# Two tokens per partition in the first six blocks: loads in rows of 384 bytes, products as 64-row tiles

## The chip, the core and the metric

The kernel runs on one core of a Trainium2 chip. The core has engines that run side by side, each with its own queue of instructions in a fixed order: PE (TensorE, matrix products into PSUM), DVE (VectorE), ACT (ScalarE), POOL (GpSimd) and SP (SyncE, which here only issues DMAs). 16 DMA engines move data between the device memory (HBM) and the on-chip memory (SBUF). The metric is the device time of one execution in microseconds (us).

## What is computed

A gated linear attention with a recurrent state, and a two-layer network on its output:

```python
for t in range(S):                       # per batch (4) and head (8); S = 768 tokens, head_dim 48
    state = alpha[t][:, None] * state + outer(k[t], v[t])
    y[t] = q[t] @ state
x = y, laid out as (4 * 768) tokens by (8 * 48) = 384 columns
h = x @ w_in                             # 384 -> 2048
g = s * relu(h) ** 2 + b
out = g @ w_out                          # 2048 -> 384
```

q, k, v and alpha are float32 of shape (4, 8, 768, 48): one head's token is a row of 48 values, 192 bytes. The output is 3072 by 384, float32.

## The kernel before

The 3072 tokens are cut into 24 blocks of C = 128 (`NBLK`), six to a batch (`NCH`). A block lies with one token on each partition and its eight heads along the free axis, in four pairs of heads (`NP`). Within a block the recurrence is written as matrix products. For block n:

- `load_a`, `load_k`, `load_q`, `load_v` (L121 to L131) fetch the block's four tensors, one DMA each of 128 x 8 pieces of 192 bytes, into rings of 8 buffers (`NLD`).
- `ln` (ACT) takes the logarithm of alpha, and `cum` (L208) sums it over the tokens with one matmul by an upper triangular matrix `U_bf`; for the first blocks (n < 5) four tiny matmuls with `ones_c` give the block's total. ACT takes the exponentials, `bi_sb` and `b_sb` (L221, L222), and for the first blocks the decay over the whole block, `blast`. For later blocks `decay` fetches that row by way of HBM (L230, L232).
- `qk` (DVE) scales k and q by them; `tr` transposes both on PE (8 matmuls), and DVE copies the result to `qkT`.
- `amat` (L254) makes the scores: 8 matmuls, one per head, 48 rows high, 128 keys by 128 queries, into two PSUM tiles. DVE multiplies each by a causal mask (`mask4`) into `am_a`, `am_b`.
- `yp` (L274) makes y: in blocks that have a predecessor in their batch 4 matmuls of q with the state `sd_sb`, then 8 matmuls of scores with v (`v_bf`, cast by POOL in `vcast`), into `y_ps`; and 4 matmuls of k with v into `p_ps`, for the new state. ACT copies y to `y_bf`.
- `st` / `state` (L329): DVE adds the state products to the decayed old state (`t1_sb`, named t_sb in the profile), POOL multiplies it by the decay (`sd_sb`, `sc_sb`).
- `xt` transposes y on PE, ACT copies it to `xd_all`.
- `mp` (L354) is the first layer in four pieces of 12 matmuls into `h_ps`, `rl` the relu on ACT, `sq` the square on DVE (`gt_all`), `mm2` (L394) the second layer in four pieces of 4 matmuls into `o_ps`. Blocks 0 to 12 are kept on the chip (`keep_sb`) until the bias is known, then stored; the later ones are stored from `out_sb`.

The order on every engine is written out by hand. A list gives the first blocks' steps one after the other (L512), with `busy`, matmuls whose result nobody reads, between them (28 in all, 128 x 512 each). They read `U_bf` and `mask4`. From block 4 on each step has a position, `at(pos, ...)`, with a block every 8 positions. The list interleaves attention of blocks 0 to 4 with the casts of the weights (`win`, `wout`) and the first layers of blocks 0 to 3.

The DMAs of the start stand in SP's queue in the order of L445 to L461: all of blocks 0 and 1, the four quarters of w_in with alpha and k of blocks 2 and 3 between them, the four parts of w_out, then blocks 4 to 7. `early` lets ACT issue q and v of blocks 2 and 3; in ACT's order that of block 2 stands behind the exponentials of block 1. Every DMA issued by SP or ACT counts on one of eight semaphores, which are dealt out in rotation over both queues; a DMA is issued only when the last one on its semaphore has landed. At the front POOL builds the triangular matrices and the masks (a memset and a select each), and DVE clears buffers.

Of the kernel before, what the change touches and what calls it, by code (L numbers as in the profile page):

```python
# [14 lines left out]
def kernel(  # L15
# [25 lines left out]
    UNITS = 5  # L41
    assert sum(GROUPS) == NBLK
# [13 lines left out]
    y_ps = ps.tile([128, 512], FP32, name="y_ps")  # L56
    p_ps = ps.tile([128, 512], FP32, name="p_ps")
# [11 lines left out]
    ones_c = sb.tile([128, 1], BF16, name="ones_c")  # L69
    ones_f = sb.tile([128, 128], FP32, name="ones_f")  # L70
# [46 lines left out]
    def src(t, n):  # L117
        b, c = n // NCH, n % NCH
        return t[b, :, c * C : (c + 1) * C, :].rearrange("h s d -> s h d")

    def load_a(n, eng=None):  # L121
        (eng or nc.sync).dma_start(out=al_sb[n % NLD], in_=src(alpha, n))  # L122

    def load_q(n, eng=None):
        (eng or nc.sync).dma_start(out=q_sb[n % NLD], in_=src(q, n))  # L125

    def load_k(n, eng=None):
        (eng or nc.sync).dma_start(out=k_sb[n % NLD], in_=src(k, n))  # L128

    def load_v(n, eng=None):  # L130
        (eng or nc.sync).dma_start(out=v_sb[n % NLD], in_=src(v, n))  # L131
# [70 lines left out]
    def ln(n):  # L202
        nc.scalar.activation(out=la_sb[n % 2][:, :, 0:48], in_=al_sb[n % NLD], func=AF.Ln)  # L203

    def vcast(n):
        nc.gpsimd.tensor_copy(out=v_bf[n % 3], in_=v_sb[n % NLD])  # L206

    def cum(n):  # L208
        la = la_sb[n % 2]
        nc.tensor.matmul(out=cum_ps, lhsT=U_bf, rhs=la[:, :, 0:48], start=True, stop=True)  # L210
        if n < NCH - 1:
# [25 lines left out]
    def qk(n):  # L237
        nc.vector.tensor_tensor(out=kb_sb[n % 3][:, :, 0:48], in0=k_sb[n % NLD], in1=bi_sb[n % 2], op=ALU.mult)  # L238
        nc.vector.tensor_tensor(out=qb_sb[n % 2][:, :, 0:48], in0=q_sb[n % NLD], in1=b_sb[n % 2], op=ALU.mult)  # L239

    def tr(n):
        for x, t in ((0, qb_sb[n % 2]), (1, kb_sb[n % 3])):
            for p in range(NP):
                nc.tensor.transpose(  # L244
                    out=t_ps[0:112, x, p, :],
# [8 lines left out]
    def amat(n):  # L254
        qkT = qkT_sb[n % 2]
        for p in range(NP):
# [9 lines left out]
        for e in range(2):  # L266
            nc.vector.tensor_tensor(out=am_sb[e][n % 2], in0=a_ps[e], in1=mask4, op=ALU.mult)  # L267
# [5 lines left out]

    def yp(n):  # L274
        c = n % NCH
# [53 lines left out]
    def state(n):  # L329
        c = n % NCH  # L330
        if c == 0:
            nc.vector.tensor_copy(out=t1_sb[0:112], in_=pst[0:112])
        else:
            nc.vector.tensor_tensor(out=t1_sb[0:112], in0=pst[0:112], in1=sc_sb[0:112], op=ALU.add)  # L334
# [256 lines left out]
```

## Time and profile before

| | |
|---|---|
| time, median of 3 runs | 200.46 us (200.07 to 201.05) |
| span of the profiled execution, first to last instruction | 198.2 us |
| what lies around the span, against the three runs | 1.9 to 2.9 us |
| PE busy | 185.2 us (93% of the span), 2440 matmuls |
| DVE busy | 150.8 us (76%) |
| ACT busy | 118.8 us (60%) |
| POOL busy | 64.2 us (32%) |
| DMA | 113,454 packets, 30.33 MB, 106,627 of them under 512 bytes |
| a load (192 KB), from issue to landing, median | 3.2 (alpha) to 4.9 us (v) |
| PE busy from 20 to 58 us | 33.7 of 38 us |
| PE busy from 60 to 120 us | 59.9 of 60 us |

The profile's own time for the profiled execution is its span; what the runs' times hold beyond it, before the first instruction and after the last, is not in the profile. A group's "busy" adds the lengths of instructions that overlap on PE, so the price of a matmul in a row of matmuls is read from the distance of two starts. An engine named with a q (SPq, ACTq) is the queue that issues its DMAs.

### The profile page before, as it was taken

The page shows a single profiled execution, that of the slowest core. Times are in us where ns is not written, and L with a number is a line of the kernel's source. Part 1 is how long each engine was busy: PE and PEld are TensorE (multiplying, and loading weights), DVE is VectorE, ACT ScalarE, POOL GpSimd, SP SyncE. Part 2 cuts the span into 40 slices and gives each one's busy share as a digit, 9 for nine tenths or more (in the row PEclk, how much of TensorE's full clock was granted, in tenths as well). Part 3 has the DMA queues.
Part 4 walks back from the last instruction along what each step waited for, and adds up shares of the span by engine and source line. Part 5 has one row for each costly group of instructions (what it writes and reads, how often), then busy time and mean ns, then how long its engine had stood idle before and what let it go on. Part 6 is the DMA issues. An engine that isn't in the chain of part 4 may idle for free.

```text
span 198.2 us, 6120 instructions
## 1 busy us (share of the span) xinstructions
PE 185.2 (93%) x2440; PEld 145.3 (73%) x2440; DVE 150.8 (76%) x296; ACT 118.8 (60%) x243; POOL 64.2 (32%) x96
## 2 busy tenths in 40 slices
PE   1999899988899999999999999999999999999994
PEld 1566587754577688888878877878888877877783
DVE  5467777867466779789877996989987999998532
ACT  3245668381675765766766677666575665664650
POOL 5142251611120136326500633623700851652000
PEclk9999999999999999999999999999999999999999
DMA  7999999999999384693968846958947953122212
GB/s 125 189 342 232 314 283 369 199 177 193 187 172 195 60 142 86 101 159 64 195 84 148 134 68 120 159 93 193 229 87 164 161 176 112 41 82 81 87 37 79
DMA packets 113454, 30.33 MB, mean 153 GB/s; under 512 B 106627, under 2 KB 111890, under 8 KB 113426
## 3 DMA queue, kind: packets, MB, share of 16 engines
q1 hardware_dynamic: 109262, 29.15, 73.7%
q10 hardware_dynamic: 4164, 0.79, 2.8%
q8 instruction: 19, 0.31, 0.7%
q14 instruction: 9, 0.07, 0.1%
HBM read 25.19 MB, written 4.74 MB: 151 GB/s over the span
## 4 chain that ended last, share of the span: by engine, by line
PE 68%; SPq 15%; DMA 10%; DVE 3%; ACT 1%; issue 1%; ACTq 0%; DVEq 0%
PE h_ps L365 25%; PE o_ps L402 25%; DMA q_sb<-in_q_dram 8%; SPq L128 5%; PE ct_ps L244 5%; SPq L147 4%; PE a_ps L259 3%; SPq L125 3%; SPq L122 2%; PE ct_ps L210 2%; PE y_ps L287 2%; PE h_ps L312 2%; DMA al_sb<-in_alpha_dram 2%; SPq L131 1%; PE a_ps L425 1%; PE y_ps L278 1%
## 5 line engine op out<-in xcount | busy, mean ns | idle before, releaser
L379 ACT ACTIVATE r_sb<-h_ps 128x512 bf16<-128x512 f32 x94 | 55.8, 597 | 39.2 <-PE h_ps L365 37.6
L365 PE MATMUL h_ps<-xd_all,w_in_bf 128*128 128x128 bf16 x1128 | 74.8, 219 | 1.5 <-ACT r_sb L379 1.1
L365 PEld LDWEIGHTS <-w_in_bf 128*128 128x128 bf16 x1152 | 69.3, 98 | 8.4 <-issue 2.3
L402 PE MATMUL o_ps<-w_out_bf,gt_all 128*128 128x384 bf16 x336 | 68.5, 326 | 1.4 <-DVE w_out_bf L160 0.7
L386 DVE TENSOR_TENSOR gt_all<-r_sb 128x512 bf16<-128x512 bf16 x96 | 45.3, 484 | 26.5 <-ACT r_sb L379 25.8
L339 POOL TENSOR_TENSOR sd_sb<-t_sb,blast 48x192 bf16<-48x192 f32 x40 | 22.5, 563 | 103.5 <-DVE t_sb L334 67.3
L402 PEld LDWEIGHTS <-gt_all 128*128 128x128 bf16 x368 | 32.5, 98 | 17.4 <-issue 1.8
L343 POOL TENSOR_TENSOR sc_sb<-t_sb,blast 112x384 f32<-112x384 f32 x16 | 21.8, 1362 | 1.3
L206 POOL CAST v_bf<-v_sb 128x384 bf16<-128x384 f32 x24 | 17.7, 744 | 12.9 <-DMA v_sb<-in_v_dram 12.7
L318 ACT ACTIVATE xd_all<-h_ps 128x384 bf16<-128x384 bf16 x24 | 11.8, 490 | 15.5 <-PE h_ps L312 15.5
L249 DVE COPY qkT<-ct_ps 112x1024 bf16<-112x1024 bf16 x24 | 16.4, 685 | 4.8 <-PE ct_ps L244 4.7
L238 DVE TENSOR_TENSOR kb_sb<-k_sb,bi_sb 128x384 bf16<-128x384 f32 x24 | 13.7, 569 | 8.3 <-ACT bi_sb L221 8.2
L267 DVE TENSOR_TENSOR am_a<-a_ps,mask 128x512 bf16<-128x512 f32 x24 | 16.4, 683 | 3.1 <-PE a_ps L259 3.1
L239 DVE TENSOR_TENSOR qb_sb<-q_sb,b_sb 128x384 bf16<-128x384 f32 x24 | 16.7, 694 | 0.0
L267 DVE TENSOR_TENSOR am_b<-a_ps,mask 128x512 bf16<-128x512 f32 x24 | 16.3, 681 | 0.0
L221 ACT ACTIVATE bi_sb<-ct_ps 128x384 f32<-128x384 f32 x24 | 11.7, 487 | 5.2 <-PE ct_ps L213 3.9
L305 ACT ACTIVATE y_bf<-y_ps 128x384 bf16<-128x384 f32 x24 | 11.7, 488 | 4.9 <-PE y_ps L287 4.8
L203 ACT ACTIVATE la_sb<-al_sb 128x384 bf16<-128x384 f32 x24 | 12.4, 516 | 3.6 <-DMA al_sb<-in_alpha_dram 3.6
L210 PE MATMUL ct_ps<-la_sb,U_bf 128*128 128x384 bf16 x24 | 8.2, 340 | 4.6 <-ACT la_sb L203 4.6
L222 ACT ACTIVATE b_sb<-ct_ps 128x384 f32<-128x384 f32 x24 | 11.9, 494 | 0.0
L244 PEld LDWEIGHTS <-qb_sb 128*112 128x112 bf16 x96 | 8.5, 136 | 4.4 <-DVE qb_sb L239 3.2
L259 PE MATMUL a_ps<-qkT 48*128 48x128 bf16 x192 | 10.2, 226 | 1.0 <-DVE qkT L249 0.4
(66 smaller groups left out, 195.0 us busy)
## 6 DMA issues: line engine op xcount, KB each, us to landing
al_sb<-in_alpha_dram SPq DMA_DIRECT2D x24, 192.0 KB, 3.2
k_sb<-in_k_dram SPq DMA_DIRECT2D x24, 192.0 KB, 3.6
q_sb<-in_q_dram SPq DMA_DIRECT2D x22, 192.0 KB, 4.7
v_sb<-in_v_dram SPq DMA_DIRECT2D x22, 192.0 KB, 4.9
w_in_st<-in_moe_w_in_dram SPq DMA_DIRECT2D x4, 768.0 KB
w_out_st<-in_moe_w_out_dram SPq DMA_DIRECT2D x4, 768.0 KB
out_dram<-w_in_st SPq DMA_DIRECT2D x13, 192.0 KB, 2.6
out_dram<-out_sb SPq DMA_DIRECT2D x10, 192.0 KB, 3.4
```

What stands on the lines that cost most here:

```text
L206: nc.gpsimd.tensor_copy(out=v_bf[n % 3], in_=v_sb[n % NLD])
L239: nc.vector.tensor_tensor(out=qb_sb[n % 2][:, :, 0:48], in0=q_sb[n % NLD], in1=b_sb[n % 2], op=ALU.mult)
L244: nc.tensor.transpose(out=t_ps[0:112, x, p, :], in_=t.rearrange("a h d -> a (h d)")[:, 128 * p : 128 * p + 112], identity=ident,)
L249: nc.vector.tensor_copy(out=qkT_sb[n % 2][0:112].rearrange("a x p t -> a (x p t)"), in_=t_ps[0:112].rearrange("a x p t -> a (x p t)"),)
L259: nc.tensor.matmul(out=a_ps[e][:, p, :], lhsT=qkT[r0 : r0 + 48, 1, p, :], rhs=qkT[r0 : r0 + 48, 0, p, :], start=True, stop=True,)
L267: nc.vector.tensor_tensor(out=am_sb[e][n % 2], in0=a_ps[e], in1=mask4, op=ALU.mult)
L339: nc.gpsimd.tensor_tensor(out=sd[r, :, d], in0=t1_sb[r, :, d], in1=bl[r].to_broadcast([48, NP, 48]), op=ALU.mult)
L343: nc.gpsimd.tensor_tensor(out=sc_sb[0:112], in0=t1_sb[0:112], in1=bl[0:112].to_broadcast([112, NP, 96]), op=ALU.mult)
L365: nc.tensor.matmul(out=hp[:, jj * N : (jj + 1) * N], lhsT=w_in_bf[:, kk, 128 * j : 128 * (j + 1)], rhs=xd_sb[g][:, kk, 0:N], start=(kk == ...
L379: nc.scalar.activation(out=rs, in_=h_of.pop((g, u)), func=AF.Relu)
L386: nc.vector.tensor_tensor(out=gt_sb[g][:, u * 512 : (u + 1) * 512], in0=rs, in1=rs, op=ALU.mult)
L402: nc.tensor.matmul(out=op[:, 0:d_model], lhsT=gt_sb[g][:, j * N + t * C : j * N + (t + 1) * C], rhs=w_out_bf[:, j, :], start=(j == 0), sto ...
```

## The change

It concerns the six blocks of the first batch (`paired(n)`: n < 6). Partition p of the lower half (0 to 63) holds tokens 2p and 2p + 1 of heads 0 to 3, partition 64 + p the same two tokens of heads 4 to 7. Two tokens of a head are neighbours in HBM, so a load's pieces are 384 bytes long and half as many; each load becomes two DMAs, one per half of the partitions, of 64 x 4 pieces. The loads that ACT issues are split in the same way, and the stores of these six blocks become two DMAs each, one for the even and one for the odd tokens.

The steps of these blocks follow the layout. The logarithm, the cast of v and the scaling read and write views with token and head exchanged. The cumulative sum of a block takes four matmuls of 192 columns with two new block-diagonal triangular matrices, `Ui_bf` and `Us_bf`, in place of one of 384; the totals still take four, of two columns. The transposes write to other places, 8 as before. The scores take 16 matmuls, each 48 rows high and 64 wide, with a mask `maskp`; y takes 16 matmuls 64 rows high in place of 8 of 128, and the new state 8 in place of 4. In all that makes 134 matmuls more, each with its load of weights. `y_ps` and `p_ps` become the two halves of one tile, `yp_ps`, which y of the paired blocks uses in both halves. At the front POOL builds `Ui_bf` and `Us_bf` first and then `ident`, `U_bf` and `mask4`; DVE makes `maskp` by 16 copies. Order and number of `busy` stay, and so does all else of the order.

```diff
-    y_ps = ps.tile([128, 512], FP32, name="y_ps")
-    p_ps = ps.tile([128, 512], FP32, name="p_ps")
+    yp_ps = ps.tile([128, 2, 512], FP32, name="yp_ps")
+    y_ps, p_ps = yp_ps[:, 0], yp_ps[:, 1]
...
+    def paired(n):
+        return n < NCH
+
+    def fetch(dst, t, n, eng):
         b, c = n // NCH, n % NCH
-        return t[b, :, c * C : (c + 1) * C, :].rearrange("h s d -> s h d")
+        rows = t[b, :, c * C : (c + 1) * C, :]
+        eng = eng or nc.sync
+        if paired(n):
+            for g in range(2):
+                eng.dma_start(
+                    out=dst[HP * g : HP * g + HP].rearrange("p (h t) d -> p h (t d)", t=2),
+                    in_=rows[4 * g : 4 * g + 4].rearrange("h (p t) d -> p h (t d)", t=2),
+                )
+        else:
+            eng.dma_start(out=dst, in_=rows.rearrange("h s d -> s h d"))
...
     def cum(n):
         la = la_sb[n % 2]
-        nc.tensor.matmul(out=cum_ps, lhsT=U_bf, rhs=la[:, :, 0:48], start=True, stop=True)
-        if n < NCH - 1:
+        if paired(n):
+            for t, w, x, first in ((1, Ui_bf, 0, True), (1, Ui_bf, 1, False), (0, Ui_bf, 0, False), (0, Us_bf, 1, False)):
+                nc.tensor.matmul(
+                    out=cum_ps[:, 192 * t : 192 * t + 192],
+                    lhsT=w,
+                    rhs=la[:, 4 * x : 4 * x + 4, 0:48],
...
     def amat(n):
         qkT = qkT_sb[n % 2]
-        for p in range(NP):
+        if paired(n):
+            for p in range(NP):
+                for g in range(2):
+                    for e in range(2):
+                        r, c = slice(64 * e, 64 * e + 48), slice(HP * g, HP * g + HP)
+                        t, i = p // 2, p % 2
+                        nc.tensor.matmul(
+                            out=a_ps[e][c, p, :],
+                            lhsT=qkT[r, 1, 2 * g + i, HP * t : HP * t + HP],
+                            rhs=qkT[r, 0, 2 * g + i, :],
...
+    def yp_paired(n):
...
+        for t in range(2):
+            for h in range(4):
+                for g in range(2):
+                    r = slice(HP * g, HP * g + HP)
+                    nc.tensor.matmul(
+                        out=yp_ps[:, g, 48 * h : 48 * h + 48],
+                        lhsT=am_sb[h % 2][n % 2][r, 2 * t + h // 2, :],
+                        rhs=v_bf[n % 3][r, 4 * t + h, :],
...
+        if c < NCH - 1:
+            for i in range(2):
+                for t in range(2):
+                    for g in range(2):
+                        r, p = slice(HP * g, HP * g + HP), 2 * t + i
+                        nc.tensor.matmul(
+                            out=yp_ps[:, g, 192 + 96 * i : 288 + 96 * i],
+                            lhsT=kb[r, 128 * p : 128 * p + 128],
+                            rhs=v_bf[n % 3][r, 2 * p : 2 * p + 2, :],
...
+        nc.scalar.activation(
+            out=y_bf[n % 2].rearrange("a (g x) -> a g x", g=2), in_=yp_ps[:, :, 0:192], func=AF.Copy
+        )
...
     def store(n, o):
-        nc.sync.dma_start(out=out[n * C : (n + 1) * C, :], in_=o)
+        rows = out[n * C : (n + 1) * C, :]
+        if not paired(n):
+            nc.sync.dma_start(out=rows, in_=o)
+            return
+        for t in range(2):
+            nc.sync.dma_start(
+                out=rows.rearrange("(p t) m -> t p m", t=2)[t], in_=o[HP * t : HP * t + HP]
+            )
...
-    make_upper_triangular(nc, U_bf, 1.0, diag=True)
+    for w, diag in ((Ui_bf, True), (Us_bf, False)):
+        nc.gpsimd.memset(w, 0.0)
+        for g in range(2):
+            r = slice(HP * g, HP * g + HP)
+            make_upper_triangular(nc, w[r, r], 1.0, diag=diag)
...
     make_identity(nc, ident)
+    make_upper_triangular(nc, U_bf, 1.0, diag=True)
     for i in range(NP):
         make_upper_triangular(nc, mask4[:, i], 1.0, diag=True)
+    for p in range(NP):
+        for t in range(2):
+            for g in range(2):
+                r = slice(HP * g, HP * g + HP)
+                w = Us_bf if p // 2 > t else Ui_bf
+                nc.vector.tensor_copy(out=maskp[r, p, t], in_=w[r, r])
```

## The prediction

> **What bounds the kernel now.** I read the page's slices first, then the waits of the first 62 us, then the PE timeline there and in the steady stage. Slices (PE busy, DMA share, 40 slices of 4.96 us):
>
> ```profile
> PE   1999899988899999999999999999999999999994
> ...
> DMA  7999999999999384693968846958947953122212
> ...
> PE 68%; SPq 15%; DMA 10%; DVE 3%; ACT 1%; issue 1%; ACTq 0%; DVEq 0%
> ```
>
> Two stages: up to about 65 us the DMA row is full and PE has holes; after that PE is full and DMA is not. The chain (third line) puts 25% of the span on SPq and DMA, all of it before 58 us, which would make the loads the bound of the first stage. The waits of engines for data don't bear this out. Of the waits in the first 62 us, these are all that end with a DMA's landing on ACT, POOL or DVE (us in total, times, longest):
>
> ```profile
> POOL v_bf L206 <- DMA v_sb<-in_v_dram: 12.7, 4, 3.9
> ...
> ACT la_sb L203 <- DMA al_sb<-in_alpha_dram: 3.6, 2, 1.8
> ...
> ACT w_in_bf L154 <- DMA w_in_st<-in_moe_w_in_dram: 0.8, 1, 0.8
> ```
>
> POOL's casts of v are early: v of block 4 lands at 41.77 and its products start at 52.37. The two waits for alpha are those of blocks 0 (3.83) and 1 (7.97); the second has 0.8 us to spare, for its cumulative sum stands behind block 0's scores on PE, which end at 9.32. From 20 to 58 us no engine but POOL waits for a load. PE idles 4.3 us of these 38, released by ACT and DVE, and is busy in all but 0.1 of the 60 us from 60 to 120. So in the first stage the fixed order on PE and the round trips PE to ACT to DVE set the pace, and each matmul added there pushes all behind it. The timeline of PE shows the price of the matmuls that the change multiplies (start, length, what; the distance of starts is the cost, lengths overlap):
>
> ```profile
> 87.77 0.18 PE L287 MATMUL y_ps<-v_bf,am_b 128*128 128x48 bf16 x1
> 87.80 0.33 PE L298 MATMUL p_ps<-v_bf,kb_sb 128*128 128x96 bf16 x4
> 88.06 0.40 PE L259 MATMUL a_ps<-qkT 48*128 48x128 bf16 x8
> 88.39 0.82 PE L402 MATMUL o_ps<-w_out_bf,gt_all 128*128 128x384 bf16 x4
> 89.05 0.33 PE L312 MATMUL h_ps<-ident,y_bf 128*128 128x128 bf16 x3
> 89.22 0.33 PE L210 MATMUL ct_ps<-la_sb,U_bf 128*128 128x384 bf16 x1
> 89.38 0.81 PE L402 MATMUL o_ps<-w_out_bf,gt_all 128*128 128x384 bf16 x4
> ```
>
> Warm prices: the 8 scores 0.33 (41 ns each), the cumulative sum 0.16, the 4 state products about 0.16, and the 8 y products, from 87.59 to 87.80, 26 ns each. Up to 14.5 us the same groups cost about double though the granted clock reads 1.00: scores 8.78 to 9.32 (0.54), cumulative sum 9.32 to 9.61 (0.29), y 11.20 to 11.55 (0.35), state 11.55 to 11.85 (0.30). At the front POOL builds the masks (start, length):
>
> ```profile
> 0.73 0.20 POOL masks.py:65 MEMSET U_bf<- 128x128 bf16 x1 [0.29 <-POOLq L575]
> 1.02 0.29 POOL masks.py:66 TENSOR_SCALAR_AFFINE_SELECT U_bf<-U_bf 128x128 bf16<-128x128 bf16 x1
> ...
> 3.56 0.29 POOL masks.py:66 TENSOR_SCALAR_AFFINE_SELECT mask<-mask 128x128 bf16<-128x128 bf16 x1
> ```
>
> Six pairs at 0.51 each end at 3.85; the first filler matmul, which reads the last mask, starts at 5.61.
>
> **The change, part by part.** The sum goes against the profiled span of 198.2 us. The three timed runs (200.07 to 201.05, median 200.46) lie 1.9 to 2.9 above it; I add what I find to the median.
>
> *Loads.* 24 loads of 1,024 pieces become 48 DMAs of 256 pieces. Issues cost 0.43 (idle queue) to 0.99 us (crowded) per load now; a half lies between 0.25 (the one-row copies of the decay) and 0.43 (a whole load), so a pair costs 0.5 to 0.9. Block 0's alpha lands 3.0 after its issue; the second half issues 0.4 later with half the pieces ahead of it, so its sum starts 0.5 earlier to 0.4 later; I take 0.2 earlier. All other loads but one group are early by the waits above, and a faster load there is worth nothing. The Trainium skill (DMA: Bandwidth & Descriptors, Rules for kernel authors) says that two transfers to disjoint partition halves serialize and are not worth making; by that the 0.2 would be a loss of about 0.4. Nothing in this profile splits a load so.
>
> *The weights behind ACT.* DMAs of SP and ACT count on eight semaphores in rotation, and a DMA issues only when the last one on its semaphore has landed. SP's wait list shows it now: k of block 3 sits 0.6 us until q of block 2, issued by ACT, lands at 17.37. With twice as many DMAs the rotation falls differently: the built program lets the second quarter of w_in wait for the first half of q of block 2, which ACT issues only after block 1's exponentials (10.15 now, about 11.2 then). It lands 2 to 5 us later (2.6 is a store's median, 7.2 was the same load behind 2 MB of other traffic), so w_in's second quarter issues at about 13.6 in place of 8.3. 768 KB at the 342 to 369 GB/s of the best slices is 2.2 us, plus about 2 us from issue to landing (1.9 for the tiny blast copies): it lands at 18.2, and up to 20.6 if it takes the 7 us that it takes now. ACT casts it now at 15.47, ahead of block 1's y_bf (16.81); queued behind that cast are y_bf, the transposes of y on PE, the first relus and ln of block 2. Block 1's y_bf goes to 18.2 + 0.1 + 0.62 = 18.9, 2.1 late.
>
> *POOL and DVE at the front.* Ahead of the filler's mask now stand two memsets (0.28 each) and four 64-wide pairs more, each between half of 0.51 and all of it: 1.6 to 2.6, so the mask is ready at 5.4 to 6.4, later still if POOL slows as it does elsewhere beside DVE (the pair of state products takes 1.08 alone and 2.21 beside DVE's casts). DVE's 16 small copies at 0.06 to 0.15 (its smallest memset and copy) plus memsets are 1.1 to 2.6, in the 2.3 us that it idles before 5.72. I take the fillers 0.5 late, the transposes of block 0 behind them as well.
>
> *PE, blocks 0 and 1 (cold).* Scores 8 to 16, y 8 to 16, state 4 to 8, one sum of 384 columns to four of 192. At one price each the additions are 0.54 + 0.35 + 0.30 + 0.29 = 1.48 per block; at pairs side by side, the sum alone, 0.29. With about two thirds for block 0, its y ends some 1.6 late, at 14 us. There the rates double, so what still stands in front of block 1's y costs half: about 0.8 comes back and block 1 adds 0.3. PE by itself would be 1.1 late at block 1's y; the late weights make it 2.1. Both run side by side, so the front costs 2.0, bounds 0.3 and 4.4.
>
> *PE, blocks 2 to 5 (warm).* At one price: 0.33 + 0.21 + 0.16 + 0.16 = 0.86, and 0.70 for block 5, which has no state. If the scores' 64-wide tiles issue at the 26 ns floor of the y row and the state halves too: 0.09 + 0.21 + 0.05 + 0.16 = 0.51. A switch between 64-row and 128-row work shows as a gap of 0.1 between the end of the state products (87.97) and the scores (88.06); two more switches make 0.2 at most. I take 0.75 per block, nearer the rows as they stand, as a stationary load goes with each: 2.8 with block 5, less 0.3 for holes of PE that some of it falls into (0.66 before 40.48 waits on a DVE cast, 0.42 and 0.58 on ACT copies around 48 to 50). 2.5, bounds 1.2 and 4.0. The fillers, 28 matmuls, stay and give nothing back.
>
> *One PSUM tile for y and state.* In the built program the state add on DVE now waits for y_bf on ACT, in every block, and y_bf for the state products. Steady rows: y_bf runs 88.22 to 88.71, the add starts at 88.71 and the state products end by 88.13, so the wait is 0.1 at most, and DVE idles 0.2 and 0.6 per block; cost nothing, 1.8 over 18 blocks if that cover goes. In blocks 2 and 3 the add shifts by 0.2 to 0.4, ahead of w_in casts that are needed 3 us later.
>
> *Stores.* Six of the kept stores become two of 64 rows: six issues at 0.33 to 0.43, from 133 us on, where SP waits 19 us in total for the adds on DVE. Hidden; 2.4 if not.
>
> Sum: 2.0 + 2.5 = 4.5 on the span, 200.46 + 4.5 is about 204.9; as the front leans on a landing that may come sooner, I say 204.7.
>
> **Rivals.** *The loads were the bound* (the chain's reading; faster). The place is SP's queue from 9 to 42 us: the twelve loads of blocks 2 to 5 that SP issues, at 0.99 each now, cost 0.76 as pairs; 2.8 us earlier, 0.2 at the front, and only the dearer sum, 0.16 x 4, stays: 200.46 - 2.4 = 198.1. It decides if engines in 20 to 58 us prove to move with the landings. For it: chain and DMA row; against it: no wait there ends with a load but POOL's.
>
> *Tiles side by side.* The halves lie in different row and column groups, so pairs could run at once, and scores, y and state cost what they cost now. Then 0.16 per warm block and about 0.3 at the front remain, if the weights are on time: 200.46 + 0.9 is 201.4. For it: scores, which alternate two row groups already, cost 41 ns against 56 for a full-height matmul (12 in 0.67). Against: each added matmul brings its own weight load, and y is at 26 ns already. The Trainium skill states this rule (TensorE: Matmul & The Clock Gate, Part 3): tiles at different row groups run concurrently, starts some 4 ns apart; and, the other way, TensorEngine Tiling, Key Properties, that changing the mode drains the engine. No row here separates them.
>
> *Late weights.* q's first half takes 5 us and w_in lands at 20.6: y_bf of block 1 is 4.5 late, and the sum 200.46 + 4.5 + 2.5 = 207.5.
>
> **How the numbers follow.** Forecast 0.60 with its own range 202.3 to 207.0 (front 0.7 to 3.5, warm blocks 1.2 to 3.0); loads the bound 0.15; side by side 0.15; late weights 0.10. Half a per cent, 1.0 us, is what a measurement of this kernel can tell from no change (its three runs span 0.98). Faster: the first rival, 0.15. Same: two fifths of the second, plus an edge of the first, 0.07. Slower: the rest, 0.78. The range 200.0 to 208.0 leaves out most of the first rival and a tail of the last.
>
> **What would show it.** Right: PE's groups of blocks 2 to 5 each longer by 0.5 to 1.1 in all; w_in's second quarter issued at 13 to 14 us with SP waiting on q; ACT's cast of it near 18; an unchanged period of 7.04 us per block after 65; fillers starting near 6.1. Wrong: PE's stage before 60 us shorter, or y of block 1 before 17.5 us, or scores at 0.33 for 16. It would also be wrong if the doubling of PE's rate, at 14.5 us now, came several us sooner or later.

## Result and profile after: 5.6% slower

| | before | changed |
|---|---|---|
| time, median | 200.26 us (199.39 to 201.05) | 211.25 us (210.62 to 211.75) |
| ratio | | 1.0555, 95% interval 1.051 to 1.060 |
| span of the profiled execution | 198.2 us | 208.8 us (its time 210.62) |
| PE busy | 185.2 us | 188.1 us |
| y_bf of block 0, 1, 2, 4 starts at | 11.77, 16.81, 25.79, 52.77 | 14.39, 22.58, 34.30, 62.84 |
| from y_bf of block 4 to the end of the span | 145.4 us | 146.0 us |

The forecast was 204.7 (200.0 to 208.0). Its direction held; the time lies 3.3 us above its upper end. Before block 4 the kernel loses 10.1 of the 10.6 us of span: 2.6 up to y_bf of block 0, 3.2 more up to block 1, 4.3 more up to block 4. From there on the two run alike, 7.04 us per block as before. Medians and ratios here and below are over fast runs; a run more than 1.5% above the fastest of its kernel is left out as slow.

The slices of the page of the changed kernel (busy tenths, 5.22 us each):

```profile
PE   0776569998989999999999999999999999999994
...
PEclk9999859999999999999999999999999999999999
DMA  3687987986899838736877457737659384322112
```

Three things are new. The DMA row starts at 3 and 6 where it stood at 7 and 9: the DMA engines are fed too slowly. PE has a hole up to 31 us. And the granted clock falls to about half in the sixth slice. The chain of work helps little: it is followed back only to 43.95 us, and so it tells nothing of the stage where the time goes. SP's timeline of the kernel before, then of the changed kernel (start, length, queue, transfer):

```profile
6.49 0.99 SPq L131 DMA_DIRECT2D v_sb<-in_v_dram  x1
7.52 1.51 SPq L142 DMA_DIRECT2D w_in_st<-in_moe_w_in_dram  x2
```

```profile
2.21 1.28 SPq L131 DMA_DIRECT2D k_sb<-in_k_dram  x2
...
10.12 1.27 SPq L131 DMA_DIRECT2D v_sb<-in_v_dram  x2
11.47 6.32 SPq L169 DMA_DIRECT2D w_in_st<-in_moe_w_in_dram  x2
```

A half costs SP 0.64 us, and blocks 0 and 1 are issued at 11.4 in place of 7.5. 96 KB per 0.64 us is 154 GB/s; from 5 to 10 us the DMA engines moved 152 (190 in the kernel before). The first two quarters of w_in then take 6.3 us to issue. SP's own waits in the first 62 us (us in total, times, longest) tell why:

```profile
SPq L131 <- DMA q_sb<-in_q_dram: 6.1, 1, 6.1
SPq L169 <- DMA q_sb<-in_q_dram: 5.3, 1, 5.3
```

L169 is w_in's second quarter: it waits on its semaphore for the first half of q of block 2, which ACT issues. SP stood at it from 12.05 us on and issued it at 17.41. The other row is k of block 3, behind ACT's q of block 3. ACT's timeline shows both ends of it:

```profile
11.66 0.69 ACTq L131 DMA_DIRECT2D q_sb<-in_q_dram  x1
...
13.04 1.31 ACTq L131 DMA_DIRECT2D v_sb<-in_v_dram  x2
14.39 0.49 ACT L386 ACTIVATE y_bf<-yp_ps 128x384 bf16<-128x384 f32 x1 [1.80 <-PE ct_ps L303]
...
22.04 0.63 ACT L181 ACTIVATE w_in_bf<-w_in_st 128x512 bf16<-128x512 f32 x1 [4.26 <-DMA w_in_st<-in_moe_w_in_dram]
22.58 0.47 ACT L386 ACTIVATE y_bf<-yp_ps 128x384 bf16<-128x384 f32 x1
```

First, ACT issues four halves from 11.66 to 14.35, and y_bf of block 0 starts right behind them; its products had been done by 12.9. Then ACT waits 4.3 us for w_in's second quarter, and y_bf of block 1 stands behind that cast. In the kernel before, the same cast came at 15.47:

```profile
15.47 0.63 ACT L154 ACTIVATE w_in_bf<-w_in_st 128x512 bf16<-128x512 f32 x1 [0.78 <-DMA w_in_st<-in_moe_w_in_dram]
```

PE pays (its timeline in the changed kernel):

```profile
16.12 0.42 PE L321 MATMUL a_ps<-qkT 48*64 48x128 bf16 x16 [0.41 <-DVE qkT L308]
...
23.11 0.34 PE L430 MATMUL h_ps<-ident,y_bf 128*128 128x128 bf16 x3 [3.56 <-ACT y_bf L386]
23.59 0.83 PE L487 MATMUL h_ps<-xd_all,w_in_bf 128*128 128x128 bf16 x12
...
25.38 1.44 PE L487 MATMUL h_ps<-xd_all,w_in_bf 128*128 128x128 bf16 x12
...
28.43 1.44 PE L487 MATMUL h_ps<-xd_all,w_in_bf 128*128 128x128 bf16 x12 [1.61 <-ACT r_sb L501]
```

It idles 3.56 us, and soon after that 12 matmuls take 1.44 us where they took 0.83; the granted clock is 0.50 from 25 to 31 us. The 16 scores, on the other hand, run from 16.12 to the next start at 16.47: 0.35, where the 8 of before took 0.33.

### The profile page after: what moved, and what is told of

It is laid out like the page before. It is cut to its first block, busy times and chain, and to the rows that moved or that the text cites. A ratio compares the mean times of both kernels' runs of the same rounds, so it can differ in the third digit from the quotient of the medians.

```text
span 208.8 us, 6454 instructions
## 1 busy us (share of the span) xinstructions
PE 188.1 (90%) x2574; PEld 148.1 (71%) x2574; DVE 154.7 (74%) x315; ACT 118.8 (57%) x243; POOL 68.8 (33%) x106
## 4 chain that ended last, share of the span: by engine, by line
PE 67%; DVE 6%; ACT 3%; issue 2%; ACTq 0%; DVEq 0%
PE o_ps L524 25%; PE h_ps L487 24%; PE ct_ps L303 4%; PE a_ps L331 3%; ACT r_sb L501 2%; PE h_ps L430 2%; PE a_ps L524 2%; DVE gt_all L508 1%; PE yp_ps L405 1%; PE ct_ps L250 1%; PE a_ps L547 1%; PE yp_ps L396 1%; PE yp_ps L416 1%; DVE w_out_bf L187 1%; ACT w_in_st L533 1%
## 5 line engine op out<-in xcount | busy, mean ns | idle before, releaser
L487 PE MATMUL h_ps<-xd_all,w_in_bf 128*128 128x128 bf16 x1128 | 76.0, 221 | 2.1 <-ACT r_sb L501 1.6
L487 PEld LDWEIGHTS <-w_in_bf 128*128 128x128 bf16 x1152 | 70.4, 99 | 9.0 <-issue 3.4
L508 DVE TENSOR_TENSOR gt_all<-r_sb 128x512 bf16<-128x512 bf16 x96 | 46.4, 497 | 24.8 <-ACT r_sb L501 24.0
L465 POOL TENSOR_TENSOR sc_sb<-t_sb,blast 112x384 f32<-112x384 f32 x16 | 23.7, 1479 | 1.3
L235 POOL CAST v_bf<-v_sb 128x384 bf16<-128x384 f32 x24 | 18.1, 760 | 10.9 <-DMA v_sb<-in_v_dram 10.7
L290 DVE TENSOR_TENSOR qb_sb<-q_sb,b_sb 128x384 bf16<-128x384 f32 x24 | 14.4, 601 | 0.0
L430 PE MATMUL h_ps<-ident,y_bf 128*128 128x128 bf16 x72 | 8.0, 220 | 4.8 <-ACT y_bf L386 4.8
L340 DVE TENSOR_TENSOR am_a<-a_ps,mask 128x512 bf16<-128x512 f32 x18 | 12.2, 680 | 0.0
L340 DVE TENSOR_TENSOR am_b<-a_ps,mask 128x512 bf16<-128x512 f32 x18 | 12.2, 679 | 0.0
L430 PEld LDWEIGHTS <-y_bf 128*128 128x128 bf16 x72 | 5.5, 98 | 8.7 <-ACT y_bf L386 5.7
L303 PE MATMUL ct_ps<-ident,qb_sb 128*112 128x128 bf16 x96 | 10.0, 229 | 1.0 <-DVE qb_sb L290 0.7
```

The costliest lines, as they stand in the source:

```text
L235: nc.gpsimd.tensor_copy(out=by_head(v_bf[n % 3], n), in_=by_token(v_sb[n % NLD], n))
L290: nc.vector.tensor_tensor(out=by_head(o[:, :, 0:48], n), in0=by_token(x[n % NLD], n), in1=by_head(w[n % 2], n), op=ALU.mult,)
L303: nc.tensor.transpose(out=o, in_=t.rearrange("a h d -> a (h d)")[:, 128 * p : 128 * p + 112], identity=ident,)
L430: nc.tensor.transpose(out=hp[:, kk * C : (kk + 1) * C], in_=y_bf[n % 2][:, 128 * kk : 128 * (kk + 1)], identity=ident,)
L465: nc.gpsimd.tensor_tensor(out=sc_sb[0:112], in0=t1_sb[0:112], in1=bl[0:112].to_broadcast([112, NP, 96]), op=ALU.mult)
L487: nc.tensor.matmul(out=hp[:, jj * N : (jj + 1) * N], lhsT=w_in_bf[:, kk, 128 * j : 128 * (j + 1)], rhs=xd_sb[g][:, kk, 0:N], start=(kk == ...
```

## The experiments

Four explanations stood against one another: the second DMA of each load, with the queues coupled through the semaphores (A); the added matmuls on PE (B); the masks and copies at the front (C); and the rival that the loads were the bound, so that long pieces should pay (D). Times are medians, ratios are to the kernel before on the same chip (median 200.1 to 200.3 us in all these runs).

### One DMA per load

```diff
-            for g in range(2):
-                eng.dma_start(
-                    out=dst[HP * g : HP * g + HP].rearrange("p (h t) d -> p h (t d)", t=2),
-                    in_=rows[4 * g : 4 * g + 4].rearrange("h (p t) d -> p h (t d)", t=2),
-                )
+            two = t[b, 4 * (c % 2) : 4 * (c % 2) + 4, 256 * (c // 2) : 256 * (c // 2) + 256, :]
+            eng.dma_start(
+                out=dst.rearrange("p (h t) d -> p h (t d)", t=2),
+                in_=two.rearrange("h (p t) d -> p h (t d)", t=2),
+            )
```

> The changed kernel with one thing undone: each load of the first six blocks is one DMA of 128 x 4 pieces of 384 bytes and not two of 64 x 4. For that a load takes four heads of 256 neighbouring tokens in place of eight heads of 128, so the first batch's outputs belong to other tokens; bytes, piece sizes and every later instruction are those of the change. Theory A (the second DMA per load is what costs: 0.64 us of SP per half, and the rotation of the semaphores that puts w_in's second quarter behind ACT's load of q): the loads of blocks 0 and 1 are issued by about 8 us, w_in's second quarter lands by about 16 and not 22, y_bf of block 1 starts at 18 to 19.5, the granted clock stays at 1.00, and the time is 201.5 to 204. Theory B (the added matmuls and the mode of the tiles cost PE the time): y_bf of block 1 may come earlier, but the distance from there to y_bf of block 4 stays near 40 us (36.0 before) and the time at 207 or more. Theory D (the loads were the bound, and long pieces pay once they come in one DMA): under 200.

204.04 us, ratio 1.0245 (1.018 to 1.031; the medians alone give 1.019). y_bf of block 1 at 17.51, granted clock 1.00 throughout. A load of 512 pieces in one DMA costs SP 0.51 us, less than one half of 256 pieces:

```profile
4.51 0.59 SPq L131 DMA_DIRECT2D v_sb<-in_v_dram  x1
5.15 1.40 SPq L169 DMA_DIRECT2D w_in_st<-in_moe_w_in_dram  x2
```

Theory A's chain held, with the time at the upper end of the range given and y_bf of block 1 half a us ahead of its own. More than half of the loss is gone with every added matmul, mask and copy still there. B fails as the main cause, and the front and PE are left with the rest.

### The old kernel with its loads split

```diff
+        parts = (slice(0, 64), slice(64, 128)) if n < NCH else (slice(0, 128),)
+        for r in parts:
+            (eng or nc.sync).dma_start(out=dst[r], in_=rows[r])
```

> The kernel before with one part of the change alone: the loads of the first six blocks are two DMAs each, partitions 0 to 63 and 64 to 127, with the old layout and pieces of 192 bytes. PE, DVE, POOL and ACT do what they do before. Theory A: the halves cost SP about 0.64 us each, w_in's second quarter is issued near 16 and lands near 21, y_bf of block 1 starts at 21 to 22.5, PE idles some 3 us and the granted clock halves; 206 to 210. If the issue price goes by the pieces (512 a half here, 256 in the change) and not by the DMA, it is later still. Theories B and C (matmuls; masks and copies at the front): 200 to 201.5, since none of these are in it.

210.61, ratio 1.0531 (1.050 to 1.056): nearly the whole loss, with the old layout and no added matmul (0.6 above the range given). A pair costs 1.31 us with 512 pieces a half and 1.28 with 256, so the price goes by the DMA. y_bf of block 1 at 22.99; the waits of ACT for w_in (us in total, times, longest) were

```profile
ACT w_in_bf L159 <- DMA w_in_st<-in_moe_w_in_dram: 6.1, 2, 3.4
```

against 0.8 before. That the split is sufficient is shown. The two parts don't add up (10.4 for the split, 3.9 for the layout, 11.0 together): while all wait for the weights, the dearer front and the longer rows of matmuls run beside that wait.

### w_in ahead of q and v of block 1

```diff
     load(0)
-    load(1)
+    load_a(1)
+    load_k(1)
...
     load_w_in(0)
     load_w_in(1)
+    load_q(1)
+    load_v(1)
```

> The changed kernel with the first two quarters of w_in ahead of q and v of block 1 in SP's queue; in the built program w_in's second quarter then waits for a half of SP's own and not for ACT's. All the halves, matmuls, masks and copies stay. Theory A: w_in lands by 16 us, q and v of block 1 by 16 to 18, y_bf of block 1 at 18.5 to 20, no hole on PE over 3 us, the granted clock stays at 1.00 and the time is 203 to 206. Theory B: the time after y_bf of block 1 is as long as in the change, 208 or more.

211.40, ratio 1.0557 (1.053 to 1.058): no gain; what I had expected of A failed. w_in is early now, but q and v of block 1 are late, and v's second half waits 3.3 us on SP for the half of q that ACT issues. From the timeline of DVE and the waits:

```profile
17.40 0.56 DVE L290 TENSOR_TENSOR qb_sb<-q_sb,b_sb 128x384 bf16<-128x384 f32 x1 [4.00 <-DMA q_sb<-in_q_dram]
```

```profile
POOL v_bf L235 <- DMA v_sb<-in_v_dram: 14.6, 3, 11.3
```

y_bf of block 1 came at 23.95. Moving a load inside the queue changes which load is late. It remains to take the coupling away.

### SP issues all early loads

```diff
     def early(n):
-        load_q(n, nc.scalar)
-        load_v(n, nc.scalar)
+        pass
...
     load_a(2)
     load_k(2)
+    load_q(2)
+    load_v(2)
```

The same for block 3.

> The changed kernel with all its halves, in which SP and not ACT issues q and v of blocks 2 and 3 (behind alpha and k of the same block), so that no DMA of SP has to wait for one that ACT has not issued yet. Theory A1 (the coupling of SP's queue to ACT's through the semaphores is what makes the weights late): w_in's second quarter is issued near 12.7 and lands by 17, y_bf of block 1 starts at 18.5 to 20, the granted clock stays at 1.00, and the time is 203.5 to 206.5. Theory A2 (the price of the halves on SP, 0.64 us each, is enough by itself): SP has issued w_out no sooner than in the change, 32 us, another load is late in place of w_in, and the time is 208 or more. Theory B (PE): 208 or more with y_bf of block 1 below 20.

205.39, ratio 1.0262 (1.022 to 1.030): A1 in the place and size given, though w_in's second quarter landed at 19.2 and not by 17. From SP's and ACT's timelines:

```profile
11.45 1.14 SPq L169 DMA_DIRECT2D w_in_st<-in_moe_w_in_dram  x2
```

```profile
19.19 0.63 ACT L181 ACTIVATE w_in_bf<-w_in_st 128x512 bf16<-128x512 f32 x1 [1.95 <-DMA w_in_st<-in_moe_w_in_dram]
```

SP issues w_in without a wait, and y_bf of block 1 is at 19.73. 5.9 of the 11 us go with the loads that ACT issues. The move takes two things away at once: the wait of SP for ACT's loads, and the time in which ACT itself stands in its issues (in the change also from 23.60 to 26.84, with bi_sb of block 2 right behind them at 26.96). No run parts the two. With both gone, halves at 0.64 us still bring w_in 3.7 us later than before. The granted clock still fell, to 0.50 from 22 to 25 us, which was not expected.

### The old kernel split by heads

```diff
-        parts = (slice(0, 64), slice(64, 128)) if n < NCH else (slice(0, 128),)
-            (eng or nc.sync).dma_start(out=dst[r], in_=rows[r])
+        parts = (slice(0, 4), slice(4, 8)) if n < NCH else (slice(0, 8),)
+            (eng or nc.sync).dma_start(out=dst[:, r], in_=rows[:, r])
```

> The kernel before with the loads of the first six blocks as two DMAs each, as in the run that split them by partitions, but split by heads: both DMAs cover all 128 partitions with 4 pieces of 192 bytes, 512 pieces each as there. If a half costs SP 0.64 us because it covers only 64 partitions: 0.4 to 0.5 each here, blocks 0 and 1 issued by 8.5 to 9.5 in place of 11.7, w_in's second quarter lands by 20 and the time is 204 to 208. If every DMA of this size costs 0.64: as there, 209.5 to 211.5. A pair of halves that costs no more than one load, 200 to 202, would leave the coupling of the queues without effect too.

209.66, ratio 1.0479 (1.043 to 1.053). A half over all 128 partitions costs 0.53 us against 0.65 over 64, with the same 512 pieces, so the number of partitions matters. The time missed its range: w_in's second quarter was cast at 17.29 and y_bf of block 1 came at 19.81, but then ACT itself stood 4.3 us in front of bi_sb, its queue held by an early load:

```profile
27.09 0.49 ACT L226 ACTIVATE bi_sb<-ct_ps 128x384 f32<-128x384 f32 x1 [4.29 <-DMA q_sb<-in_q_dram]
```

y_bf of block 2 came at 34.30, as in the change.

### Long pieces alone, in the old layout

The loads of the first run above, in the kernel before; nothing else.

> The kernel before with one thing of the change: the loads of the first six blocks fetch pieces of 384 bytes, 512 to a load, in one DMA each. The steps stay as they were and take each piece as two heads of one token, so the first batch's outputs are those of other tokens. Theory D (the loads were the bound of the first stage): SP issues each load in 0.5 us in place of 0.4 to 1.0 and all of blocks 0 and 1 by 5.2 in place of 7.5; the time falls below 199. If the engines' order is the bound, as the forecast had it: 199.5 to 200.5, within 0.5% of before.

199.33, ratio 0.9942 (0.992 to 0.997), between the two ranges given. SP issues blocks 0 and 1 by 5.3 in place of 7.5, and the kernel gains 0.3 to 0.85%. From y_bf of block 1 to that of block 4 it takes 35.97 us, before it took 35.96: nothing of the gain comes from the loads of blocks 2 to 5, where theory D had placed it. It arises ahead of block 1. Of the 1.65 us by which the profiled execution reaches y_bf of block 1 sooner, a part is not the loads': PE's rate doubled near 9 us there and near 15 in the kernel before (its scores from 14.44 to 14.98 still took 0.54), which is left to chance (last section). Long pieces are worth about one us here; the change as written can't have it, because it pays for each piece saved with a second DMA.

### A shorter front

On the kernel with one DMA per load:

```diff
-    for i in range(NP):
-        make_upper_triangular(nc, mask4[:, i], 1.0, diag=True)
-    for p in range(NP):
...
-                nc.vector.tensor_copy(out=maskp[r, p, t], in_=w[r, r])
+    make_upper_triangular(nc, mask4[:, 0], 1.0, diag=True)
     nc.vector.memset(ones_g, 0.0)
...
+    for g in range(2):
+        r = slice(HP * g, HP * g + HP)
+        for o, w in (
+            (maskp[r, 0:2].rearrange("a p t s -> a (p t) s"), Ui_bf),
+            (maskp[r, 2:4, 1], Ui_bf),
+            (maskp[r, 2:4, 0], Us_bf),
+        ):
+            one = w[r, r].rearrange("a (x s) -> a x s", x=1)
+            nc.vector.tensor_copy(out=o, in_=one.to_broadcast([HP, o.shape[1], HP]))
+    nc.vector.tensor_copy(out=mask4[:, 1:4], in_=mask4[:, 0:1].to_broadcast([128, 3, 128]))
```

> The kernel with one DMA per paired load (the outputs of its first batch belong to other tokens, as there), with a shorter front: DVE clears ones_g, ones_f and sd_sb ahead of the mask, makes maskp with 6 copies that repeat a 64 x 64 triangle in place of 16 copies, and copies three of the four parts of mask4, so that POOL builds one in place of four. There the totals of block 0 waited 1.45 us for ones_g behind DVE's copies, the fillers started at 7.44 and y_bf of block 0 at 13.25. Theory C (the front is the larger part of what is left of the loss, 3.3 us of span): fillers near 6, y_bf of block 0 at 11.9 to 12.5, and 1 to 2 us less than that kernel, 202 to 203.4. If the loss is PE's added matmuls from block 2 on: y_bf of block 0 comes as early, the gain is lost before block 4, and the time stays at 204 or more.

205.12, ratio 1.0242 (1.020 to 1.029): no gain, though the front did all that was expected. Fillers start at 5.60, y_bf of block 0 at 11.14, of block 1 at 15.32, ahead of the kernel before. Then ACT's timeline reads

```profile
17.55 0.37 ACTq L131 DMA_DIRECT2D q_sb<-in_q_dram  x1
21.55 0.37 ACTq L131 DMA_DIRECT2D v_sb<-in_v_dram  x1
22.05 0.49 ACT L272 ACTIVATE bi_sb<-ct_ps 128x384 f32<-128x384 f32 x1 [4.47 <-DMA v_sb<-in_v_dram]
```

In this program v of block 3 counts on the semaphore of v of block 2, which had not landed. ACT stands 4 us in the issue, PE idles 4.55, the clock halves, and y_bf of block 2 comes at 30.57 (26.68 without the short front). The second reading of the expectation, PE's matmuls, is not what took the gain; neither reading had this.

### Short front and SP's loads

One DMA per load, and the same two edits:

> One DMA per paired load and the short front (the first batch's outputs belong to other tokens), and q and v of blocks 2 and 3 issued by SP in place of ACT. In the run with the short front y_bf of block 1 started at 15.32, 1.5 ahead of the kernel before, and then ACT stood 4.5 us ahead of bi_sb, because its issue of v of block 3 waited for v of block 2 to land; y_bf of block 2 came at 30.57. If that wait is what took the gain: y_bf of block 2 at 24 to 25.5, granted clock 1.00, and 200.5 to 202.5. If the layout's own work from block 2 on took it: 203 or more. Set against the next-but-two run, which has the same loads with the old layout, the difference is the price of the added matmuls and of the shared PSUM tile: 1.5 to 3 us by the rows (0.17 for the sum, 0.1 for y and about 0.3 for y_bf behind the state products, per block), 2.5 or more at one price per matmul.

201.37, ratio 1.0042 (0.999 to 1.009), the granted clock at 1.00: the wait was what took the gain. From y_bf of block 1 to that of block 2 it takes 9.18 in place of 15.25 us. The starts themselves lie later than expected, block 2 at 26.23: PE's rate doubled later in this execution (y_bf of block 0 at 12.55, 11.14 above). With two halves per load, the layout's own tokens:

> The changed kernel (two DMAs of 64 partitions per load, its own tokens) with the short front and with q and v of blocks 2 and 3 issued by SP. Without the short front this stood at 205.4, y_bf of block 1 at 19.7 behind w_in's second quarter, which landed at 19.2. Theory A2 (the halves' 0.64 us on SP set the pace once the queues are uncoupled): the front gains nothing, y_bf of block 1 stays at 19 to 20, and the time at 204.5 to 206. Theory C (the front sets it): 202.5 to 204.

203.93, ratio 1.0171 (1.008 to 1.026). y_bf of block 1 at 19.61, as without the short front, which is A2's mark; the time lies below A2's range and in C's. So the front does not reach block 1. By the traces the span is 1.5 us shorter than without the short front: 0.1 up to y_bf of block 1, 1.0 from there to block 4, 0.4 behind it. In the middle part the clock differs. The windows from 22 to 25 us, first without, then with the short front (length, PE busy and matmuls, PEld, DVE, ACT, POOL, granted clock, DMA share, GB/s):

```profile
22.00:25.00 3.00, 2.74 (x28) 2.58 (x27) 1.67 (x3) 1.91 (x5) 1.78 (x3) 0.50 0.91 299
```

```profile
22.00:25.00 3.00, 2.13 (x36) 1.92 (x35) 1.85 (x3) 2.37 (x6) 1.28 (x3) 1.00 1.01 347
```

The timed runs agree: the mean granted clock is 0.990 to 0.992 in all four without the short front; with it, it is 1.00 in the three at 203.8 to 204.0 us and 0.982 in the one at 206.44, which widens the interval. So most of the 1.5 us go with the clock; why it stayed up here, after a gap on PE of 1.15 us in place of 1.65, is open. With the next run, the partner with the old layout:

> The kernel before with the loads of the first six blocks in pieces of 384 bytes, one DMA each (the first batch's outputs are those of other tokens), and with q and v of blocks 2 and 3 issued by SP: the partner with the old layout to the run with the short front and SP's loads. If the coupling of the queues costs the kernel before nothing: 198.5 to 200, as without this move (199.3). If SP's longer queue delays the weights: 200.5 or more.

198.31, ratio 0.9875 (0.980 to 0.995). Its y_bf starts agree with those of the run without this move within 0.05 us: in the kernel before, the coupling costs nothing. The layout costs 3.1 us against this partner, by medians (with the ends of both intervals, 0.9 to 5.8): just above the 1.5 to 3 that the rows gave, and in the 2.5 or more of one price per matmul, which this interval can't rule out. The spans of the two profiled executions differ by 3.8. 1.9 of it arises up to y_bf of block 1, with the front and PE's late rate in it; from there to y_bf of block 4 it is 37.69 against 35.96 us, 1.7 for three blocks.

### One PSUM tile alone

```diff
-    y_ps = ps.tile([128, 512], FP32, name="y_ps")
-    p_ps = ps.tile([128, 512], FP32, name="p_ps")
+    yp_ps = ps.tile([128, 2, 512], FP32, name="yp_ps")
+    y_ps, p_ps = yp_ps[:, 0], yp_ps[:, 1]
```

> The kernel before with y_ps and p_ps as the two halves of one PSUM tile, and nothing else. The forecast gave this no cost: the state add then waits for y_bf, and y_bf for the state products, 0.1 us of it uncovered at most in the steady blocks. If so: 200 to 200.8. If the wait counts in each of the first blocks (0.3 us, as y_bf stood 0.2 behind the state products with the layout): 201 to 202. If it counts in the 18 later blocks too: over 202.

200.76, ratio 1.0011 (0.996 to 1.006): in the range of "no cost", but too wide to tell nothing from one us. The traces, one execution of each, tell more: from y_bf of block 1 to that of block 4 it takes 36.95 in place of 35.96 us, and from there to the end 145.5 in place of 145.4. New in the waits from 20 to 56 us:

```profile
DVE t_sb L334 <- ACT y_bf L305: 0.8, 2, 0.5
```

So by these traces the shared tile costs 1.0 us over the first blocks of the old layout; if it costs the same in the new one, it is 1.0 of the layout's 1.7. Behind that add DVE has casts of w_in in block 2 and four squares in block 3; that they carry the delay on is read from the order, not tried. The matmuls are then left with 0.7 for three blocks. In the run with one DMA, the short front and SP's loads, block 3's sum reads

```profile
29.03 0.41 PE L241 MATMUL ct_ps<-la_sb,Ui_bf 128*128 128x192 bf16 x3
29.28 0.25 PE L241 MATMUL ct_ps<-la_sb,Us_bf 128*128 128x192 bf16 x1
29.36 0.32 PE L255 MATMUL ct_ps<-ones_g,la_sb 128*112 128x2 bf16 x4
```

0.33 from the first start to the totals, against 0.16 before. That is the one group whose price doubled.

### The halved clock

The change with 16 more fillers in PE's hole:

```diff
-            (win, 0), (win, 1), (busy, 5), (yp, 1), (mr, 0, 0), (st, 1), (busy, 1), (xt, 1), (ln, 2), (early, 3), (mp, 0, 1),
+            (win, 0), (win, 1), (busy, 5), (yp, 1), (mr, 0, 0), (st, 1), (busy, 17), (xt, 1), (ln, 2), (early, 3), (mp, 0, 1),
```

> The changed kernel with 16 more filler matmuls (0.22 us each warm, 3.5 in all) on PE between block 1's products and the transposes of its y, where PE idles 3.6 us for the late weights. Theory A with the clock as its second half: y_bf of block 1 stays at 22.5, the granted clock stays at 1.00 between 24 and 32 us where the change shows 0.50, and the distance from y_bf of block 1 to that of block 4 falls from 40.3 to 37.5 to 38.5; 208 to 209.5. If the halved clock is no cause but only goes along with the loss: 211 to 212. If PE had no room there: 213 or more.

210.82, ratio 1.0531 (1.050 to 1.057). The clock stayed at 1.00, and from y_bf of block 1 to that of block 4 it took 38.31 in place of 40.26 us; but w_in landed 1.4 us later in this execution, and the time fell between the two readings. Once more, beside the change on the same chip:

> The changed kernel with 16 more fillers, once more. If the halved clock costs the change about 2 us: from y_bf of block 1 to that of block 4 in 38 to 38.5 again (40.3 in the change), and a time 1 to 2.5 below the change on the same chip, if w_in lands at the same time in both. If SP's later loads set the pace of block 3 with or without the clock: the same time within 0.7 us, as before.

> The changed kernel as it is, once more, to stand beside the run with 16 fillers on the same chip: 210.5 to 212, granted clock 0.50 between 25 and 31 us, y_bf of block 1 at 22 to 24.

210.28, ratio 1.0507 (1.048 to 1.053), against 211.43, ratio 1.0553 (1.051 to 1.059). The stretch took 38.11 against 39.94 us. But w_in did not land at the same time: y_bf of block 1 came at 23.05 with the fillers and at 24.63, outside its range, without. The windows from 25 to 31 us, first of the run with fillers, then of the change (PE busy and matmuls, PEld, DVE, ACT, POOL, granted clock, DMA share, GB/s):

```profile
25.00:31.00 6.00, 3.78 (x60) 2.92 (x61) 2.39 (x5) 3.02 (x7) 1.73 (x3) 1.00 1.02 285
```

```profile
25.00:31.00 6.00, 5.13 (x45) 4.80 (x46) 2.25 (x5) 3.40 (x9) 2.39 (x4) 0.50 0.98 288
```

60 matmuls in 3.78 us busy against 45 in 5.13. The stretch gets 1.8 to 2.0 us shorter with the clock kept, twice; the time is 1.2 lower by medians, with intervals that overlap. The ten timed runs of the change point the same way: six with a mean granted clock of 0.976 took 211.0 to 212.3 us, three with 0.983 or 0.984 took 210.1 to 211.3, and one with 0.992 took 209.8. About one to two of the 11 us go with the clock. The other place where it had fallen, 7 fillers in the run with SP's loads:

> The changed kernel with q and v of blocks 2 and 3 issued by SP (205.39, y_bf of block 1 at 19.73, of block 2 at 29.24, of block 4 at 57.48; granted clock 0.50 from 22 to 25 us) and 7 more fillers, 1.5 us warm, ahead of the transposes of block 1's y, where PE idles 1.65 us. If the clock is the cause of what follows: granted clock 1.00, y_bf of block 2 at 28.2 to 28.6, the time 0.7 to 1.5 lower, 204 to 204.8. If it only goes along: y_bf of block 2 at 29 or later and 205 to 206.

205.56, ratio 1.0260 (1.023 to 1.029), the same time, with the clock at 1.00 and y_bf of block 2 at 29.78 in place of 29.24: the second reading. But these fillers did not fit into the hole. In this execution y_bf of block 0 came 1.1 us later, the fillers ran until 21.60, and the transposes behind them began 1.8 us after y_bf of block 1, 0.5 without them. So here they cost about what the clock gave back. Where the clock stayed up without fillers, in the run with halves and the short front, y_bf of block 2 follows that of block 1 after 8.71 us, with the halved clock after 9.51.

## Why the prediction fell short

Step by step, as the prediction put it:

- *What bounds the kernel.* Held. The old kernel's stage from block 1 to 4 doesn't move with faster loads (35.97 against 35.96 us), so the chain's 25% on SPq and DMA was no bound there. Held only where a margin is left, though: delay one load by 5 us and it is the bound.
- *Loads: "a half lies between 0.25 and 0.43 us".* Wrong, and the first failed step. 0.64 lies outside both ends. Those ends came from a one-row copy and from a whole load, and a load on half of the partitions was like neither. The rows of the profile offered no price, and 0.99, a crowded whole load, should have been the upper end. The Trainium skill (DMA: Bandwidth & Descriptors, Rules for kernel authors), which the forecast weighed at 0.4 us, advises against two transfers to partition halves because they share the same engines. The runs agree with the advice; what they show as the cause is SP's issue.
- *The same price on ACT* was missing from the sum. Four halves hold ACT from 11.66 to 14.35, and y_bf of block 0 behind them.
- *Weights behind ACT: 2.1 late at y_bf of block 1.* Mechanism right, term mis-sized: 5.8. SP stood ready at w_in's second quarter at 12.05, so SP's own lateness did not set its issue; q did. ACT issued it at 11.66 (11.2 forecast), and its first half took 5.7 us to land where the sum had 2.4 and the text 2 to 5. The 7.2 us that the same load took in the kernel before had been set aside. So the second quarter was issued at 17.41 (13.6 forecast) and landed at 22.0 against 18.2, beyond even the 20.6 of the late-weights rival. (The forecast's own terms, 13.6, 2.2 and 2, add up to 17.8.) This is the step that failed in size, and it holds the largest part of the loss.
- *What follows a hole on PE* had no term. 3.56 us idle, then the clock at 0.50: one to two us go with it.
- *PE, blocks 0 and 1 (cold): 1.1 late at block 1's y.* Near: y's products are done 1.1 us late in block 0 and 1.5 in block 1. But luck is in it. In this execution PE's rate doubled near 10.7 us and not near 15, which the forecast had named as a sign of being wrong; in the second profiled execution of the change, where it had not doubled by 14 us, block 0's products are done 2.3 late.
- *PE, blocks 2 to 5: 2.5.* Too dear. Scores took 0.35 against 0.33, y comes in pairs 25 ns apart, and only the sum doubled: 0.7 for three blocks, if the tile's 1.0 is taken off the 1.7. The side-by-side rival was right here. The Trainium skill (TensorE: Matmul & The Clock Gate, Part 3) says that tiles on different row groups run at the same time; the pairs agree.
- *One PSUM tile: "cost nothing".* Wrong by the traces: 1.0 us in blocks 2 to 4 of the old layout. The forecast saw the add of blocks 2 and 3 shift by 0.2 to 0.4 us (the one in block 2 waits 0.5) and trusted the 3 us that the casts of w_in had to spare; y_bf of block 4 came later all the same. In the steady blocks it held.
- *Front: fillers 0.5 late.* They were 1.8 late (7.40), as each of the 16 copies took 0.18 us and ones_g stood behind them. With the weights later still, no run shows that it reached the end of the change.
- *Stores, steady period.* Held: 0.6 us more from block 4 to the end, 7.04 per block.

By medians the kernel runs down a ladder: 211.3 the change, 205.4 with SP's loads, 203.9 with a short front too, 201.4 with one DMA per load, 198.3 with the old layout, and 200.2 with the old pieces. In this order of steps about six us go with ACT's early loads (SP's wait for them and ACT's own issues), about two and a half with the halves' issue price, about three with the layout, less one to two that the long pieces bring. The step from 205.4 to 203.9 goes mostly with the clock. Of the 4.3 us lost between blocks 1 and 4, 1.8 to 2.0 go with the clock and 1.7 with the layout; the rest, some 0.6, is not assigned.

## What to carry over

Before you split a DMA, price the issue on each queue that carries it, and write down for the new count of DMAs which transfer each one's semaphore waits for, above all across queues: here one early load on ACT held SP, and another held ACT. Where a step shifts, follow what is queued behind it on its engine, in the blocks where the shift occurs; the cover in the steady blocks does not tell. When a fixed order loses a load's margin, the loss grows behind it, through whatever stands in the same queue and through PE's clock.

## What the hardware showed

- A load on 64 partitions costs SP 0.64 us whether it has 256 or 512 pieces. On 128 partitions 512 pieces cost 0.53 as 192 bytes each and 0.51 as 384. Why half the partitions cost more was not tried.
- The granted clock does not follow the length of one gap alone. It halved after 3.56 us idle; in the run with w_in first it stayed at 1.00 after 3.67 us idle at 18.0 and fell at 30.2, with 1.92 as the longest gap shortly before; with SP's loads it fell at 22 after 1.65. The Trainium skill (TensorE: Matmul & The Clock Gate, Part 1) states that the rate halves after an idle window of about 3.4 us and that this window runs freely; by the second part a gap of this length can miss one, but the falls after 1.92 and 1.65 us do not fit the first.
- When PE's rate doubles at the start differs between executions of one program. In two profiled executions of the change, the 16 scores of block 0 took 0.39 us in one and 0.58 in the other, where fillers still ran at half rate at 14 us; y_bf of block 0 came at 14.39 and 15.03. In two kernels with the short front, one DMA per load in both, y_bf of block 0 came at 11.14 and 12.55 with the same start up to 8.77. So about one us of a profiled front is chance, and only medians of several runs tell such a difference.
